# One PSUM tile per bank and attention outputs in halves, in a planned attention and token/channel mixing kernel

## The chip, the cores and the metric

The kernel runs on one core of one Trainium2 chip. The metric is device time in microseconds (us), as the median of several runs. A profile's span is about two us shorter than the time of its run. Engines in the profile: PE is TensorE, PEld its weight loads, DVE is VectorE, ACT is ScalarE, POOL is GpSimd, SP issues DMAs (POOL issues the loads).

## The reference, cut to what matters

```python
# 8 batches, 8 heads, 1024 rows, head size 64, projection 64
k_proj = einsum('ks,bhsd->bhkd', E, k);  v_proj = einsum('ks,bhsd->bhkd', F, v)
x = softmax(q @ k_proj.T / 8) @ v_proj             # [8, 1024, 512] after joining heads
h = relu(x.T @ w_tok1) @ w_tok2                    # token mixing, hidden 256
u = x + h.T
out = u + relu(u @ w_ch1) @ w_ch2                  # channel mixing, hidden 1536
```

In the program, `token1` and `token2` are the two products of the token mixing; `kp` and `vb` are the copies of the projected k and v, `x_sb` holds x and `uT` the transpose of u. The two channel products take most of TensorE's work. The kernel computes them with seven block products in place of eight (Strassen's scheme), so partial results live in PSUM banks that are seeded by a copy and added to.

## The kernel before: the parts that matter

A planner written in Python orders the whole program before it is built. It has three streams that take PSUM banks: U (the up products), D (the down products) and F (the "front": projections, scores, attention outputs "attend", token mixing). U and D share banks 0 to 5, F has banks 6 and 7. The planner knows eight single banks. The program declares four tiles of two banks each:

```python
pairs = [ps.tile([P, 2, S2], F32, tag=f"ps{i}", name=f"ps{i}") for i in range(4)]

def bank(b):
    t = pairs[b.at[0] // 2]
    return t if b.n == 2 else t[:, b.at[0] % 2, :]
```

The waits between engines are added later by the framework, which follows the accesses of each tile.

`attend` writes a head's output to both front banks and VectorE normalises it in one reciprocal and one product:

```python
def attend(h, due):
    bk = Bank("F", 2)                       # both front banks
    ...                                     # 4 matmuls, 130 columns each
    nc.vector.reciprocal(out=rdn, in_=view()[:, :, :, D])
    nc.vector.tensor_tensor(out=x_sb[...], in0=view()[:, :, :, 0:D],   # 512 columns
                            in1=rdn[..., None].to_broadcast([P, 2, 4, D]), op=ALU.mult)
```

The projections of k and v stand in one bank and leave it in four copies, `kp` twice and `vb` twice, shared between VectorE and ScalarE.

The softmax here doesn't subtract the row's maximum and nothing guards it: scores larger than these inputs give would overflow.

Of the kernel before, what the change touches and what calls it, by code (L numbers as in the profile page):

```python
# [25 lines left out]
class Bank:  # L26


    def __init__(self, stream, n=1):
        self.stream, self.n, self.jobs, self.at = stream, n, [], None  # L30
        self.read, self.write = [], []


class Planner:
# [35 lines left out]
    def plan(self):  # L70
# [30 lines left out]

        def home(b, now):

            if held[b.stream] + b.n > self.caps[b.stream]:
                return None
            if b.stream != "F" and turn[b.stream][0] is not b:
                return None
            best = None
            if b.n == 1:
                spots = [(i,) for i in ((6, 7) if b.stream == "F" else range(6))]  # L110
            else:
                spots = [(6, 7)]
            for s in spots:
                t = [bank_free[i] for i in s]
                if None in t:
                    continue
                mates = 0
                c = (max(now, max(t)), -mates, max(t), s)
                if best is None or c < best:
                    best = c  # L120
            return best

        while any(can.values()):
            pick = None
            for e, js in can.items():
                f = free.get(e, 0.0)
                cands = []
                for j in js:
                    t = max(f, est[j.n])
                    spot = None  # L130
                    if j.takes:
                        h = home(j.takes[0], t)
                        if h is None:
                            continue
                        t, spot = h[0], h[3]
                    cands.append((t, j.prio, j.n, j, spot))
                if not cands:
                    continue
                t0 = min(c[0] for c in cands) + 0.02
                c = min((c for c in cands if c[0] <= t0), key=lambda c: (c[1], c[2]))  # L140
                if pick is None or c[0] < pick[0]:
                    pick = c
            if pick is None:
                raise RuntimeError("no job can go on", [(j.eng, j.fn.__qualname__, j.prio) for js in can.values() for j in js][:20], held, bank_free)
            t, _, _, j, spot = pick
            can[j.eng].remove(j)
            j.start, j.end, j.full = t, t + j.lat, t + j.lat + 0.03
            free[j.eng] = t + j.occ
            if j.takes:
                b = j.takes[0]  # L150
                b.at = spot
                turn[b.stream].remove(b)
                held[b.stream] += b.n
                for i in spot:
                    bank_free[i] = None
            for b in j.banks:
                left[id(b)] -= 1
                if not left[id(b)]:
                    held[b.stream] -= b.n
                    for i in b.at:  # L160
                        bank_free[i] = max(x.end for x in b.jobs) + 0.1
            order.append(j)
            for s in j.next:
                waiting[s.n] -= 1
                if not waiting[s.n]:
                    open_(s)
# [5 lines left out]
def kernel(  # L172
# [13 lines left out]
    nc = tc.nc  # L186
# [40 lines left out]
    def tile_of(shape, dtype, name):  # L227
        return sb.tile(shape, dtype, tag=name, name=name)

    pairs = [ps.tile([P, 2, S2], F32, tag=f"ps{i}", name=f"ps{i}") for i in range(4)]  # L230

    def bank(b):

        t = pairs[b.at[0] // 2]
        return t if b.n == 2 else t[:, b.at[0] % 2, :]

    ident = tile_of([P, P], BF16, "ident")
    make_identity(nc, ident)
# [25 lines left out]
    S_t = [tile_of([P, 4, 2, 2, P], BF16, f"S{i}") for i in range(2)]  # L264
    G_t = [tile_of([P, 7, C2, 2 * P], BF16, f"G{i}") for i in range(2)]
    a_t = [tile_of([P, S2], BF16, f"a{i}") for i in range(4)]
    rdn_t = [tile_of([P, 2, 4], F32, f"rdn{i}") for i in range(4)]
    ub_t = [tile_of([P, 2, 2 * P], F32, f"ub{i}") for i in range(2)]
    ua_t = [tile_of([P, 2, 2 * P], F32, f"ua{i}") for i in range(2)]
    g21_t = [tile_of([P, 2, 2 * P], BF16, f"g21{i}") for i in range(2)]  # L270
# [98 lines left out]
    def warm(i):  # L369
        pe(  # L370
            1, 512,
            lambda: blank(pairs[i // 2][:, i % 2, :]),
            prio=-200, writes=[("bank", i)],
        )

# [50 lines left out]
    def kv_proj(b, h0, hn, due):  # L426
        hs = slice(h0, h0 + hn)
        heads = range(h0, h0 + hn)
        bk = Bank("F")

        def view():
            return bank(bk).rearrange("p (h d) -> p h d", d=D)

        def mm(lo, hi):
            t = view()
            for si in range(lo, hi):
                a, z = si == 0, si == NSI - 1
                nc.tensor.matmul(  # L438
                    t[0:KP, 0:hn], ET_sb[:, si, :], k_sb[:, hs, si, :], start=a, stop=z
                )  # L440
                nc.tensor.matmul(
                    t[KP : 2 * KP, 0:hn], FT_sb[:, si, :], v_sb[:, hs, si, :], start=a, stop=z
                )

        cols = hn * D
        reads = ["ET", "FT"] + [(n, h) for n in "kv" for h in heads]
        pl.add(
            "PE", 8 * max(cols, 128) / 2400 + 0.22, 8 * max(cols, 128) / 2400 + 0.22,
            lambda: mm(0, NSI), reads=reads, takes=[bk], prio=due,
            after=[("vb", i, h) for i in range(2) for h in heads],  # L450
        )
        e = [
            lambda: nc.vector.tensor_copy(out=kp[:, hs, 0, :], in_=view()[0:KP, 0:hn]),
            lambda: nc.scalar.copy(out=kp[:, hs, 1, :], in_=view()[0:KP, 0:hn]),
            lambda: nc.vector.tensor_copy(
                out=vb[KP : 2 * KP, hs, 1, 0:D], in_=view()[KP : 2 * KP, 0:hn]
            ),
            lambda: nc.scalar.copy(out=vb[0:KP, hs, 0, 0:D], in_=view()[KP : 2 * KP, 0:hn]),
        ]
        dve(cols, e[0], writes=[("kp", 0, h) for h in heads], uses=[bk])  # L460
        act(cols, e[1], writes=[("kp", 1, h) for h in heads], uses=[bk])
        dve(cols, e[2], writes=[("vb", 1, h) for h in heads], uses=[bk])
        act(cols, e[3], writes=[("vb", 0, h) for h in heads], uses=[bk])

    def k_transpose(h0, hn, due):
# [77 lines left out]
            writes=[("a", h % 4)], uses=[bk],  # L543
        )

    def attend(h, due):
        bk = Bank("F", 2)

        def view():
            return bank(bk)[:, :, 0 : 4 * D1].rearrange("p n (c d) -> p n c d", d=D1)  # L550

        def mm():
            for j in range(NJ):
                nc.tensor.matmul(  # L554
                    view()[:, j // 2, 2 * (j % 2) : 2 * (j % 2) + 2].rearrange("p c d -> p (c d)"),
                    a_t[h % 4][:, j * P : (j + 1) * P],
                    vb[:, h].rearrange("k c d -> k (c d)"), start=True, stop=True,
                )

        pe(  # L560
            NJ, 130, mm, reads=[("a", h % 4), ("vb", 0, h), ("vb", 1, h)], takes=[bk], prio=due,
            after=[("x", h)],
        )
        rdn = rdn_t[h % 4]
        pl.add(
            "DVE", 0.23, 0.21,
            lambda: nc.vector.reciprocal(out=rdn, in_=view()[:, :, :, D]),
            writes=[("rdn", h % 4)], uses=[bk],
        )
        dve(  # L570
            512,
            lambda: nc.vector.tensor_tensor(  # L572
                out=x_sb[:, :, h * D : (h + 1) * D].rearrange("p (n c) d -> p n c d", n=2),
                in0=view()[:, :, :, 0:D],
                in1=rdn[:, :, :, None].to_broadcast([P, 2, 4, D]),
                op=ALU.mult,
            ),
            reads=[("rdn", h % 4)], writes=[("x", h)], uses=[bk],
        )

    def token1(t, due):
# [8 lines left out]

        for part in range(2):
            pe(
                4, 512, lambda part=part: mm(part), reads=["wt1"] + [("x", h) for h in range(H)],
                takes=[bk] if part == 0 else [], uses=[bk] if part else [], prio=due + 0.9 * part,
            )
        act(
# [4 lines left out]
    def token2(b, si, due):  # L601
        bk = Bank("F")

        def mm():
# [12 lines left out]
            lambda: nc.vector.tensor_add(  # L617
                out=u_t[b % 2][:, si, :], in0=bank(bk), in1=x_sb[:, si, :]
            ),
            reads=[("x", h) for h in range(H)], writes=[("u", b % 2, si)], uses=[bk],  # L620
        )
        if si % NJ == NJ - 1:
            i = si // NJ
# [30 lines left out]
    def token1_pair(hp, due):  # L654
# [13 lines left out]
        for t in range(TC):  # L668
            pe(
                NSI, 128, lambda t=t: mm(t),  # L670
                reads=["wt1", ("x", 2 * hp), ("x", 2 * hp + 1)],
                takes=[bk] if t == 0 else [], uses=[bk] if t else [], prio=due,
            )
        act(
# [5 lines left out]
    def token2_pair(hp, i, due):  # L680
# [6 lines left out]
        def mm():  # L687
# [14 lines left out]
            lambda: nc.vector.tensor_add(  # L702
                out=u_t[0][:, rows, cols], in0=view(), in1=x_sb[:, rows, cols]
            ),
            reads=[("x", 2 * hp), ("x", 2 * hp + 1)], writes=[("up", hp, i)], uses=[bk],
        )

    def u_transpose_pe(hp, i, due):
# [230 lines left out]
    for hp in range(HP):  # L939
        q_transpose_pe(hp, due + 8 + 2 * hp)  # L940
        scores(2 * hp, due + 9 + 2 * hp)
        scores(2 * hp + 1, due + 9 + 2 * hp)
        attend(2 * hp, due + 10 + 2 * hp)
        attend(2 * hp + 1, due + 10 + 2 * hp)
    for hp in range(HP):
        token1_pair(hp, due + 20 + hp)
    for i in range(2):
# [4 lines left out]
    def front(b, begin, end):  # L952
# [4 lines left out]
        for h in range(H):  # L957
            if h + 2 < H:
                units.append((0.4, lambda t, h=h: scores(h + 2, t)))
            units.append((0.5, lambda t, h=h: attend(h, t)))  # L960
        for n in range(TC):
            units.append((1.8, lambda t, n=n: token1(n, t)))
        for si in range(NSI):
# [60 lines left out]
```

## Time and profile before

| | before |
|---|---|
| time, median | 560.0 us |
| PE / DVE / ACT busy | 82 / 58 / 42% |
| idle gaps of PE | 100.2 us (558.8 - 458.6) |
| one steady batch | 58.3 us (first token1 matmul of one batch to that of the next, mean of six) |

The page of before: engine busy time, then the clock granted to TensorE in 40 slices of the span, in tenths (9 is full or nearly so).

```profile
span 558.8 us, 9128 instructions
...
PE 458.6 (82%) x3692; PEld 346.7 (62%) x3692; DVE 325.7 (58%) x656; ACT 234.9 (42%) x428; POOL 106.7 (19%) x122
...
PE   5555467888789989888888898989899889988995
...
PEclk8567577998799999999999999999999999999998
```

PE is never full for long, and in the first sixth it is about half idle.

The windows view of before: the first 90 us, and one steady batch. Columns are the length, the busy time of each engine with its instruction count, the granted clock, the DMA share and GB/s.

```profile
0.00:90.00 90.00, 50.62 (x396) 35.20 (x397) 35.49 (x79) 20.00 (x42) 28.24 (x44) 0.67 0.94 153
235.50:294.80 59.30, 51.08 (x423) 39.16 (x422) 38.23 (x75) 27.52 (x49) 11.77 (x12) 1.00 0.68 122
```

In a steady batch 8.2 of 59.3 us are gaps of PE.

The waits view of before, PE alone: who waited, for whom, us in total, times, longest.

```profile
PE ps L554 <- DVE x_sb L572: 9.6, 12, 2.5
PE ps L475 <- DVE vb L455: 8.6, 7, 2.3
PE ps L869 <- ACT G L796: 7.5, 10, 1.7
PE ps L606 <- DVE u L617: 5.4, 15, 0.6
...
PE ps L869 <- ACT ps L815: 3.3, 8, 0.7
```

L869 is a down product, L815 the copy that seeds an up bank. The timeline of before shows one such wait (start, length, engine, line; in brackets the idle time before and what ended it):

```profile
272.79 0.60 PE L775 MATMUL ps<-uT,wT 128*128 128x256 bf16 x4
...
273.48 0.57 ACT L815 COPY ps<-ps 128x512 f32<-128x512 f32 x1 [0.78 <-PE ps L775]
274.10 0.82 PE L869 MATMUL ps<-wT,G 128*128 128x256 bf16 x6 [0.71 <-ACT ps L815]
```

By the program, this copy reads bank 4 and this down product writes bank 5, the other bank of the pair. The tile makes the wait, not the data (e2 below makes each bank a tile, leaves the plan and is 73.9 us faster). I call it a neighbour wait below. The program of before has 277 waits of PE on an instruction that shares a pair tile with it but no bank; read out of the program and set against the trace, they end 62.9 us of PE's gaps. (A recount that takes in the shortest gaps gives 279 waits and 65.1 us.)

### The profile page before, as it was taken

How to read it: one execution, taken by the hardware profiler on the slowest of the kernel's cores; microseconds unless marked ns; L12 is line 12 of the kernel's file. 1: busy time of each engine (PE TensorE's matmuls, PEld its weight loads, DVE VectorE, ACT ScalarE, POOL GpSimd, SP SyncE). 2: the span in 40 equal slices, each digit the busy share in tenths (PEclk: the TensorE clock that was granted, in tenths of full speed). 3: DMA queues.
4: the chain of work that ended last, by engine and by line, in shares of the span. 5: the costliest groups of instructions: out<-in, count | busy, mean ns of one | idle time of the engine just before them, and what ended most of it. 6: DMA issues, size and time to landing. Idle time of an engine off the chain costs nothing.

```text
span 558.8 us, 9128 instructions
## 1 busy us (share of the span) xinstructions
PE 458.6 (82%) x3692; PEld 346.7 (62%) x3692; DVE 325.7 (58%) x656; ACT 234.9 (42%) x428; POOL 106.7 (19%) x122
## 2 busy tenths in 40 slices
PE   5555467888789989888888898989899889988995
PEld 3424434655566667666766677667776676767874
DVE  2354434674476766656674658476856666655551
ACT  1222025542364366435543465346543653344541
POOL 7440030022021122104030312121101010011022
PEclk8567577998799999999999999999999999999998
DMA  8999529625945299637954497429632301222111
GB/s 134 206 201 206 99 47 187 107 39 89 227 87 126 39 174 167 109 80 121 182 99 93 76 178 161 114 38 192 116 109 39 113 1 76 39 35 80 77 76 76
DMA packets 93674, 61.67 MB, mean 110 GB/s; under 512 B 59840, under 2 KB 89024, under 8 KB 93632
## 3 DMA queue, kind: packets, MB, share of 16 engines
q0 software_dynamic: 30784, 29.63, 34.6%
q1 hardware_dynamic: 62848, 31.46, 23.7%
q8 instruction: 29, 0.48, 0.3%
q14 instruction: 13, 0.11, 0.1%
HBM read 59.24 MB, written 16.78 MB: 136 GB/s over the span
## 4 chain that ended last, share of the span: by engine, by line
PE 52%; DVE 20%; ACT 13%; DMA 10%; issue 4%; POOL 0%; DVEq 0%; ACTq 0%; POOLq 0%
PE ps L869 17%; PE ps L775 16%; DMA uT<-u 9%; PE ps L606 4%; PE ps L586 4%; DVE u L617 4%; DVE x_sb L572 2%; PE ps L438 2%; PE ps L533 2%; ACT ps L815 2%; DVE g L756 2%; DVE S L645 2%; ACT G L796 2%; DVE G L809 2%; DVE G L756 2%
## 5 line engine op out<-in xcount | busy, mean ns | idle before, releaser
L869 PEld LDWEIGHTS <-G 128*128 128x128 bf16 x1344 | 131.1, 98 | 46.4 <-issue 27.4
L869 PE MATMUL ps<-wc_sb,G 128*128 128x256 bf16 x768 | 104.7, 273 | 13.0 <-ACT G L796 6.1
L796 ACT ACTIVATE G<-ps 128x512 bf16<-128x512 f32 x96 | 57.4, 598 | 100.5 <-PE ps L775 92.4
L775 PEld LDWEIGHTS <-wc_sb 128*128 128x128 bf16 x768 | 74.5, 99 | 38.0 <-issue 22.3
L869 PE MATMUL ps<-wT,G 128*128 128x256 bf16 x576 | 78.8, 274 | 5.5 <-ACT ps L907 1.4
L775 PEld LDWEIGHTS <-wT 128*128 128x128 bf16 x576 | 56.7, 99 | 24.9 <-issue 13.7
L775 PE MATMUL ps<-uT,wc_sb 128*128 128x256 bf16 x384 | 59.8, 280 | 8.3 <-DVE g L756 3.5
L901 POOL TENSOR_TENSOR db<-db,u 128x512 f32<-128x512 f32 x16 | 19.1, 1191 | 237.8 <-ACT db L899 237.8
L617 DVE TENSOR_TENSOR u<-ps,x_sb 128x512 bf16<-128x512 f32 x56 | 37.5, 689 | 42.2 <-PE ps L606 40.3
L775 PE MATMUL ps<-S,wc_sb 128*128 128x256 bf16 x384 | 58.4, 275 | 3.6 <-DVE G L756 1.9
L901 POOL TENSOR_TENSOR o<-o,u 128x512 f32<-128x512 f32 x32 | 37.1, 1160 | 123.1 <-ACT o L899 117.7
L775 PE MATMUL ps<-S,wT 128*128 128x256 bf16 x384 | 57.0, 278 | 3.8 <-ACT ps L907 1.0
L756 DVE CUSTOM_DVE_ANT_0 g<-ps,ub 128x512 bf16<-128x512 f32 x48 | 33.0, 688 | 39.1 <-PE ps L775 12.7
L756 DVE CUSTOM_DVE_ANT_0 G<-ps,ua 128x512 bf16<-128x512 f32 x48 | 33.0, 688 | 37.1 <-ACT ua L802 25.6
L542 ACT ACTIVATE a<-ps 128x512 bf16<-128x512 f32 x64 | 36.5, 600 | 24.4 <-PE ps L533 24.4
L572 DVE TENSOR_TENSOR x_sb<-ps,rdn 128x512 bf16<-128x512 f32 x64 | 44.2, 691 | 2.0
L809 DVE TENSOR_TENSOR G<-G 128x512 bf16<-128x512 bf16 x96 | 43.4, 452 | 2.5
L802 ACT COPY ua<-ps 128x512 f32<-128x512 f32 x48 | 28.2, 588 | 32.9 <-PE ps L775 27.0
L606 PE MATMUL ps<-hT_sb,wt_sb 128*128 128x512 bf16 x112 | 32.5, 385 | 8.0 <-DVE u L617 5.4
L554 PE MATMUL ps<-vb,a 128*128 128x130 bf16 x256 | 26.2, 228 | 12.1 <-DVE x_sb L572 9.6
L815 ACT COPY ps<-ps 128x512 f32<-128x512 f32 x48 | 27.7, 578 | 17.4 <-PE ps L775 8.7
L802 ACT COPY ub<-ps 128x512 f32<-128x512 f32 x48 | 28.1, 585 | 10.9 <-PE ps L869 4.4
(72 smaller groups left out, 522.8 us busy)
## 6 DMA issues: line engine op xcount, KB each, us to landing
out_dram<-o SPq DMA_DIRECT2D x32, 512.0 KB, 3.3
k_sb<-in_k_dram POOLq DMA_DIRECT2D x14, 512.0 KB, 7.3
v_sb<-in_v_dram POOLq DMA_DIRECT2D x14, 512.0 KB, 9.3
q_sb<-in_q_dram POOLq DMA_DIRECT2D x14, 512.0 KB, 7.6
wc_sb<-in_moe_w_ch_dram POOLq DMA_DIRECT2D x6, 256.0 KB, 12.6
wc_sb<-in_moe_w_ch_dram POOLq DMA_DIRECT2D x4, 384.0 KB, 12.0
k_sb<-in_k_dram POOLq DMA_DIRECT2D x4, 256.0 KB, 7.6
v_sb<-in_v_dram POOLq DMA_DIRECT2D x4, 256.0 KB, 8.2
```

The lines of the kernel that those rows point to most:

```text
L542: lambda: nc.scalar.activation(out=a_t[h % 4], in_=bank(bk), func=ACT.Exp, scale=scale),
L572: lambda: nc.vector.tensor_tensor(out=x_sb[:, :, h * D : (h + 1) * D].rearrange("p (n c) d -> p n c d", n=2), in0=view()[:, :, :, 0:D], in ...
L606: nc.tensor.matmul(bank(bk), wt2_sb[:, t, si::NSI], hT_sb[:, t, :], start=(t == 0), stop=(t == TC - 1),)
L617: lambda: nc.vector.tensor_add(out=u_t[b % 2][:, si, :], in0=bank(bk), in1=x_sb[:, si, :]),
L756: nc.vector._custom_dve(TENSOR_ADD_SAT, out=out, in0=in0, in1=in1, s0=FMAX, s1=0.0)
L775: nc.tensor.matmul(t[:, c, :], w1_of(n, dd, 2 * m + c), a_of(j, n, dd), start=(n in (1, 7) and c == 0 and dd == 0), stop=(c == 1 and dd == 1),
L796: lambda: nc.scalar.activation(out=G[:, n, cs], in_=view(src), func=ACT.Relu),
L802: 512, lambda: nc.scalar.copy(out=dst, in_=view("y")), writes=[(name, s % 2)],
L809: 512, lambda: f(out=G[:, n, cs], in0=in0, in1=in1), ps=False, reads=deps,
L815: 512, lambda: nc.scalar.copy(out=view("y"), in_=view("x")), takes=[bk["y"]],
L869: nc.tensor.matmul(view(X_OF[n])[:, t, :], G[:, G_OF[n], cc, t * P : (t + 1) * P], w2_of(n, cc), start=(n in (1, 7) and t == 0 and cc == 0 ...
L901: 512, lambda: nc.gpsimd.tensor_add(out=dst, in0=dst, in1=u_of(sh, dh)),
```

## The change

Every bank becomes a tile of its own. `attend` is cut into two halves that take one bank each. The two copies of `kp` go to VectorE and the two of `vb` to ScalarE.

```diff
-    pairs = [ps.tile([P, 2, S2], F32, tag=f"ps{i}", name=f"ps{i}") for i in range(4)]
+    banks = [ps.tile([P, S2], F32, tag=f"ps{i}", name=f"ps{i}") for i in range(8)]
     def bank(b):
-        t = pairs[b.at[0] // 2]
-        return t if b.n == 2 else t[:, b.at[0] % 2, :]
+        return banks[b.at]
 ...                                    # kv_proj
-            lambda: nc.scalar.copy(out=kp[:, hs, 1, :], in_=view()[0:KP, 0:hn]),
-            lambda: nc.vector.tensor_copy(
+            lambda: nc.vector.tensor_copy(out=kp[:, hs, 1, :], in_=view()[0:KP, 0:hn]),
+            lambda: nc.scalar.copy(
                 out=vb[KP : 2 * KP, hs, 1, 0:D], in_=view()[KP : 2 * KP, 0:hn]
 ...
-    def attend(h, due):
-        bk = Bank("F", 2)
+    def attend(h, half, due):
+        bk = Bank("F")
 ...                                    # 2 matmuls, a reciprocal of 4, a product of 256 columns
-            512,
+            256,
-                out=x_sb[:, :, h * D : (h + 1) * D].rearrange("p (n c) d -> p n c d", n=2),
+                out=x_sb[:, 4 * half : 4 * half + 4, h * D : (h + 1) * D],
 ...                                    # readers of x name the halves they need;
 ...                                    # the planner loses its two-bank case
```

More of the change, by code (lines that the diff above doesn't have):

```diff
@@ L26, with __init__ @@
 class Bank:
-    def __init__(self, stream, n=1):
-        self.stream, self.n, self.jobs, self.at = stream, n, [], None
+    def __init__(self, stream):
+        self.stream, self.jobs, self.at = stream, [], None
         self.read, self.write = [], []
@@ L102, in home @@
         def home(b, now):
-            if held[b.stream] + b.n > self.caps[b.stream]:
+            if held[b.stream] == self.caps[b.stream]:
                 return None
@@ L108, in home @@
             best = None
-            if b.n == 1:
-                spots = [(i,) for i in ((6, 7) if b.stream == "F" else range(6))]
-            else:
-                spots = [(6, 7)]
-            for s in spots:
-                t = [bank_free[i] for i in s]
-                if None in t:
-                    continue
-                mates = 0
-                c = (max(now, max(t)), -mates, max(t), s)
-                if best is None or c < best:
-                    best = c
+            for i in (6, 7) if b.stream == "F" else range(6):
+                t = bank_free[i]
+                if t is not None and (best is None or (max(now, t), t, i) < best):
+                    best = (max(now, t), t, i)
             return best
@@ L134, in plan @@
                             continue
-                        t, spot = h[0], h[3]
+                        t, spot = h[0], h[2]
                     cands.append((t, j.prio, j.n, j, spot))
@@ L152, in plan @@
                 turn[b.stream].remove(b)
-                held[b.stream] += b.n
-                for i in spot:
-                    bank_free[i] = None
+                held[b.stream] += 1
+                bank_free[spot] = None
             for b in j.banks:
@@ L158, in plan @@
                 if not left[id(b)]:
-                    held[b.stream] -= b.n
-                    for i in b.at:
-                        bank_free[i] = max(x.end for x in b.jobs) + 0.1
+                    held[b.stream] -= 1
+                    bank_free[b.at] = max(x.end for x in b.jobs) + 0.1
             order.append(j)
@@ L266 @@
     a_t = [tile_of([P, S2], BF16, f"a{i}") for i in range(4)]
-    rdn_t = [tile_of([P, 2, 4], F32, f"rdn{i}") for i in range(4)]
+    rdn_t = [tile_of([P, 4], F32, f"rdn{i}") for i in range(4)]
     ub_t = [tile_of([P, 2, 2 * P], F32, f"ub{i}") for i in range(2)]
@@ L371, in warm @@
             1, 512,
-            lambda: blank(pairs[i // 2][:, i % 2, :]),
+            lambda: blank(banks[i]),
             prio=-200, writes=[("bank", i)],
@@ L460, in kv_proj @@
         dve(cols, e[0], writes=[("kp", 0, h) for h in heads], uses=[bk])
-        act(cols, e[1], writes=[("kp", 1, h) for h in heads], uses=[bk])
-        dve(cols, e[2], writes=[("vb", 1, h) for h in heads], uses=[bk])
+        dve(cols, e[1], writes=[("kp", 1, h) for h in heads], uses=[bk])
+        act(cols, e[2], writes=[("vb", 1, h) for h in heads], uses=[bk])
         act(cols, e[3], writes=[("vb", 0, h) for h in heads], uses=[bk])
@@ L544, in scores @@
         )
-    def attend(h, due):
-        bk = Bank("F", 2)
+    def attend(h, half, due):
+        bk = Bank("F")
+        rdn = rdn_t[2 * (h % 2) + half]
         def view():
-            return bank(bk)[:, :, 0 : 4 * D1].rearrange("p n (c d) -> p n c d", d=D1)
+            return bank(bk)[:, 0 : 4 * D1].rearrange("p (c d) -> p c d", d=D1)
         def mm():
-            for j in range(NJ):
+            for jj in range(2):
+                j = 2 * half + jj
                 nc.tensor.matmul(
-                    view()[:, j // 2, 2 * (j % 2) : 2 * (j % 2) + 2].rearrange("p c d -> p (c d)"),
+                    view()[:, 2 * jj : 2 * jj + 2].rearrange("p c d -> p (c d)"),
                     a_t[h % 4][:, j * P : (j + 1) * P],
@@ L558, in mm @@
                 )
+        key = ("rdn", 2 * (h % 2) + half)
         pe(
-            NJ, 130, mm, reads=[("a", h % 4), ("vb", 0, h), ("vb", 1, h)], takes=[bk], prio=due,
-            after=[("x", h)],
+            2, 130, mm, reads=[("a", h % 4), ("vb", 0, h), ("vb", 1, h)], takes=[bk], prio=due,
+            after=[("x", h, half)],
         )
-        rdn = rdn_t[h % 4]
         pl.add(
-            "DVE", 0.23, 0.21,
-            lambda: nc.vector.reciprocal(out=rdn, in_=view()[:, :, :, D]),
-            writes=[("rdn", h % 4)], uses=[bk],
+            "DVE", 0.14, 0.18, lambda: nc.vector.reciprocal(out=rdn, in_=view()[:, :, D]),
+            writes=[key], uses=[bk],
         )
         dve(
-            512,
+            256,
             lambda: nc.vector.tensor_tensor(
-                out=x_sb[:, :, h * D : (h + 1) * D].rearrange("p (n c) d -> p n c d", n=2),
-                in0=view()[:, :, :, 0:D],
-                in1=rdn[:, :, :, None].to_broadcast([P, 2, 4, D]),
+                out=x_sb[:, 4 * half : 4 * half + 4, h * D : (h + 1) * D],
+                in0=view()[:, :, 0:D],
+                in1=rdn[:, :, None].to_broadcast([P, 4, D]),
                 op=ALU.mult,
             ),
-            reads=[("rdn", h % 4)], writes=[("x", h)], uses=[bk],
+            reads=[key], writes=[("x", h, half)], uses=[bk],
         )
@@ L592, in token1 @@
             pe(
-                4, 512, lambda part=part: mm(part), reads=["wt1"] + [("x", h) for h in range(H)],
+                4, 512, lambda part=part: mm(part), reads=["wt1"] + [("x", h, part) for h in range(H)],
                 takes=[bk] if part == 0 else [], uses=[bk] if part else [], prio=due + 0.9 * part,
@@ L619, in token2 @@
             ),
-            reads=[("x", h) for h in range(H)], writes=[("u", b % 2, si)], uses=[bk],
+            reads=[("x", h, si // NJ) for h in range(H)], writes=[("u", b % 2, si)], uses=[bk],
         )
@@ L670, in token1_pair @@
                 NSI, 128, lambda t=t: mm(t),
-                reads=["wt1", ("x", 2 * hp), ("x", 2 * hp + 1)],
+                reads=["wt1"] + [("x", 2 * hp + h, n) for h in range(2) for n in range(2)],
                 takes=[bk] if t == 0 else [], uses=[bk] if t else [], prio=due,
@@ L704, in token2_pair @@
             ),
-            reads=[("x", 2 * hp), ("x", 2 * hp + 1)], writes=[("up", hp, i)], uses=[bk],
+            reads=[("x", 2 * hp, i), ("x", 2 * hp + 1, i)], writes=[("up", hp, i)], uses=[bk],
         )
@@ L942 @@
         scores(2 * hp + 1, due + 9 + 2 * hp)
-        attend(2 * hp, due + 10 + 2 * hp)
-        attend(2 * hp + 1, due + 10 + 2 * hp)
+        for h in (2 * hp, 2 * hp + 1):
+            for half in range(2):
+                attend(h, half, due + 10 + 2 * hp)
     for hp in range(HP):
@@ L959, in front @@
                 units.append((0.4, lambda t, h=h: scores(h + 2, t)))
-            units.append((0.5, lambda t, h=h: attend(h, t)))
+            for half in range(2):
+                units.append((0.25, lambda t, h=h, half=half: attend(h, half, t)))
         for n in range(TC):
```

## The prediction

The recorded text is cut in three places: an estimate of the VectorE work that the halves add, the marks that followed from it, and a sentence on banks, none of which a run then on record showed. No term of the sum is cut: 560 - 54 - 5 = 501 stands, and a quarter taken off the gain of 59 us leaves 44 and so 516; the estimate had entered only as one reason for that quarter.

> **What bounds the kernel now.** TensorE with its stalls. The page gives PE 82% busy of a 558.8 us span, VectorE 58%, ScalarE 42%. The windows view shows a steady state: every 59-60 us stretch (one batch) from 149 to 446 us holds 52 to 55 us of PE work, 37 to 40 of VectorE, 28 to 29 of ScalarE. The first 90 us hold only 51 us of PE work. PE's idle gaps sum to about 94 us.
>
> I set the trace against the waits in the program of the kernel before, and asked which PSUM bank the waiting instruction and the awaited one touch. Of 448 waits of PE over PSUM, 277 are on an instruction that touches only the *other* bank of the same two-bank tile. By traced idle time, 62.9 us of PE's gaps (124 of them) end with such a neighbour-bank wait, 22.0 us with a real one. Example in the timeline: at 274.10 us a down product had idled 0.71 us until a ScalarE copy (an up bank's seed) ended, of which it uses nothing. The waits view has the largest forms: k transpose behind the vb eviction (8.6 us, 7 times), down products behind relu G (7.5), token2 behind a neighbour's u eviction (5.4).
>
> [...]
>
> **What the change does.** One tile per bank removes the neighbour waits on all engines. With all else at its traced time, real dependencies would leave 8.6 of the 62.9 us: 14.5 us go before 90 us, 39.7 after. Each stop also costs a refill (6 matmuls take 0.82 us in a lone group, 18 take 2.14: roughly 0.1 us): about 5 us more.
>
> Attend halves take one bank each, not both, so scores and attends overlap. Cost: 128 reciprocals and 128 products on VectorE for 64 and 64. A 512-column product takes 691 ns, a reciprocal 202[...].
>
> kv eviction: two VectorE reads, then two on ScalarE, so the k transpose starts after about 1.4 us instead of 2.7.
>
> **Sum.** First order: 560 - 54 - 5 = 501. Not all is kept: at 53-54 us a batch VectorE is some 75% loaded, in-order queues and two F banks form new real waits, the DMA transposes stay (9-11 us, on the chain once a batch), and the start (DMA 93% busy before 90 us) can shorten only by 6-10 us. I expect about three quarters, 44 us. **516 us, 80% range 498 to 537.** Faster by over 2%: 0.94, within 2%: 0.05, slower: 0.01.
>
> **What would show it.** Steady batches of 53-55 us; PE gaps down to 45-55 us, hardly any on a bank that the waiter doesn't touch; the first batch's products starting 5-10 us earlier;[...] matmul counts unchanged.
>
> **What would make it wrong.** New real waits of PE on VectorE (attend halves, two F banks) that eat the gain; the planner's new order, which I can't see; a start bound by its loads; or neighbour waits that hid slack, so that gaps only move.

## More of the kernel before

"Half clock" means a stretch in which the profile shows a granted TensorE clock of 0.5.

The order of each engine's instructions is the plan's, and the trace of before shows that order: its 3692 matmuls, its 651 VectorE and its 427 ScalarE instructions (memsets and the table load left out) stand, line for line, as in the built program.

## The result, and the profile after

| | before | after |
|---|---|---|
| time, median | 560.0 us | 475.7 us (473.4 to 480.1, 4 runs) |
| ratio | | 0.850 (95% interval 0.843 to 0.857) |
| idle gaps of PE | 100.2 us | 46.7 us |
| one steady batch | 58.3 us | 50.3 us |

A ratio here is the mean time of one kernel's fast runs over that of the other's of the same rounds, so it is not quite the ratio of the medians quoted beside it. The time lies 22 us below the predicted range; the predicted gain was 44 us and the measured one is 84.

The page of after:

```profile
span 471.6 us, 9198 instructions
...
PE 424.9 (90%) x3665; PEld 338.9 (72%) x3692; DVE 326.7 (69%) x784; ACT 235.3 (50%) x428; POOL 107.2 (23%) x122
...
PE   4757889992999989999999999999999999999994
...
PEclk8576999997999999999999999999999999999999
```

The gaps fell by 53.5 us. The other 33.7 us came off PE's *busy* time, although all 3692 matmuls are still run (their weight loads are counted in full; 27 matmul records are missing in this trace, and a run of the same speed that has them all, e4 below, shows 31.2 us less busy and 56.3 us less idle). That is the surprise to explain.

The windows view of after, for the same two stretches:

```profile
0.00:90.00 90.00, 68.50 (x627) 51.35 (x631) 58.12 (x157) 37.97 (x76) 32.06 (x48) 0.85 1.14 183
237.10:289.30 52.20, 50.00 (x430) 40.08 (x432) 39.19 (x94) 28.74 (x51) 11.05 (x12) 1.00 0.74 142
```

The gaps of PE in a steady batch are 2.2 us now. By 90 us PE has done 627 matmuls where it had done 396. The transfers speed up too, 183 GB/s for 153, so they had not been at their limit in the start. (The DMA share of this view is no ceiling either: it was 0.94 and is 1.14.)

The waits view of after, PE alone:

```profile
PE ps L765 <- DMA uT<-u: 8.5, 1, 8.5
PE ps L464 <- DVE kp L443: 7.6, 9, 1.3
PE ps L522 <- DVE x_sb L562: 5.0, 8, 1.8
PE ps L545 <- DVE x_sb L562: 4.7, 11, 0.9
```

The waits of products (L765, L859, the old L775 and L869) on ScalarE and VectorE are nearly gone (32 us in all before, 2.8 after, 5.7 in e4), and the program has no neighbour wait left. The timeline shows a seed copy (L805, the old L815) and a product in the neighbouring bank; by the program this copy reads bank 5 and this product writes bank 4:

```profile
249.31 0.57 ACT L805 COPY ps<-ps 128x512 f32<-128x512 f32 x1
...
249.57 0.60 PE L765 MATMUL ps<-uT,wT 128*128 128x256 bf16 x4
```

The product starts in the middle of the copy. The groups of attend's VectorE work, before and then after (busy, mean ns of one, idle time before and its causes):

```profile
L572 DVE TENSOR_TENSOR x_sb<-ps,rdn 128x512 bf16<-128x512 f32 x64 | 44.2, 691 | 2.0
...
L567 DVE RECIPROCAL rdn<-ps 128x8 f32<-128x8 f32 x64 | 13.0, 202 | 15.6 <-PE ps L554 15.3 <-ACT ps L815 0.3
```

```profile
L562 DVE TENSOR_TENSOR x_sb<-ps,rdn 128x256 bf16<-128x256 f32 x128 | 50.8, 415 | 0.9
...
L557 DVE RECIPROCAL rdn<-ps 128x4 f32<-128x4 f32 x128 | 21.6, 175 | 15.9 <-PE ps L545 13.8 <-ACT a L531 1.1 <-ACT ua L792 0.8
```

Count times mean: 57.1 us before, 75.5 after, so +18.4. VectorE's busy time as the page gives it, a union of overlapping records, rises only from 325.7 to 326.7; the plain sum of all its records rises by 16, from 352 to 368.

### Where busy time can hide a stop

The groups of both kernels say that a 256-column matmul is recorded for 273 ns. The timeline of before shows six matmuls after which PE stops, and six that run straight into the next ones:

```profile
280.24 0.82 PE L869 MATMUL ps<-wc_sb,G 128*128 128x256 bf16 x6
...
282.16 0.60 PE L775 MATMUL ps<-S,wc_sb 128*128 128x256 bf16 x4 [1.10 <-DVE G L756]
...
282.82 0.82 PE L869 MATMUL ps<-wc_sb,G 128*128 128x256 bf16 x6
...
283.48 0.60 PE L775 MATMUL ps<-uT,wT 128*128 128x256 bf16 x4
```

Both sixes are recorded for 0.82 us, but in the second the next matmul starts 0.66 us after the first of the six. The chain of waits of after (start, length, what) counts a group only up to the next start:

```profile
87.60 0.66 PE ps L859 x6
...
418.65 1.31 PE ps L859 x12
```

Twelve in 1.31 us are 109 ns each, and six are 0.66 us. In the six that stop, the record of the last one runs on for 165 ns (273 - 108) after the next matmul could have started. When PE stops, this tail counts as busy. The stop above cost 1.26 us (1.92 - 0.66), of which the profile shows 1.10 as idle. A stop that shows a gap is therefore its visible gap *plus* 165 ns; a stop shorter than the tail shows no gap at all. (The profiler models the ends of matmuls, so the split into gap and tail rests on its model; their sum rests on starts alone.)

So I made an account of every trace from the *starts* of successive matmuls: issue time at full clock, what it takes longer in stretches at half clock, visible gaps, and the rest, which is hidden in busy time. A stop is any start over 40 ns late. The projections of k and v need care: their matmuls start in pairs, in before most often 3 ns apart (31 ns in the median) and the next pair some 213 ns later, and this is their normal pace. (A first account took some 49 of these pairs in each trace for stops of about 0.21 us each; this table is made without them, and the differences between the kernels hardly changed. The 18.6 us in the expectation of i1 are of the first account.) Traces with all 3692 matmuls are used; for the kernel after, the run with the kv copies put back stands in, whose time is the same (474.1 us, below).

| kernel | stops | with a visible gap | issue | more at half clock | visible gaps | hidden | hidden per stop with a gap |
|---|---|---|---|---|---|---|---|
| before | 248 | 191 | 401.6 | 18.2 | 91.7 | 38.5 | 0.168 |
| six stream banks split | 137 | 91 | 401.4 | 17.8 | 62.6 | 21.2 | 0.170 |
| two front banks split | 232 | 169 | 401.5 | 14.0 | 72.3 | 35.2 | 0.166 |
| all banks split, attend whole | 155 | 63 | 402.2 | 8.5 | 41.7 | 20.7 | 0.177 |
| after (kv put back) | 125 | 71 | 401.7 | 7.0 | 35.4 | 18.3 | 0.171 |
| after on pair tiles | 297 | 211 | 401.7 | 12.1 | 99.6 | 45.3 | 0.170 |

All in us. The kernels of the middle rows are the experiments that follow. From before to after: visible gaps -56.3, hidden -20.2, half clock -11.1, issue unchanged. Hidden time and half clock sum to 31.3 us, which is what PE's busy time fell by.

### The profile page after: what moved, and what is told of

It is laid out like the page before. It is cut to its first block, busy times and chain, and to the rows that moved or that the text cites. A ratio compares the mean times of both kernels' runs of the same rounds, so it can differ in the third digit from the quotient of the medians.

```text
span 471.6 us, 9198 instructions
## 1 busy us (share of the span) xinstructions
PE 424.9 (90%) x3665; PEld 338.9 (72%) x3692; DVE 326.7 (69%) x784; ACT 235.3 (50%) x428; POOL 107.2 (23%) x122
## 4 chain that ended last, share of the span: by engine, by line
PE 63%; DVE 16%; DMA 13%; ACT 3%; issue 2%; POOL 2%; DVEq 0%; POOLq 0%; ACTq 0%
PE ps L765 23%; PE ps L859 22%; DMA uT<-u 11%; PE ps L576 5%; PE ps L596 4%; DVE S L635 3%; DVE G L799 3%; DVE x_sb L562 2%; DMA q_sb<-in_q_dram 2%; PE ps L545 2%; PE ps L427 2%; PE ps L522 2%; PE ps L653 1%; DVE G L746 1%; DVE u L607 1%
## 5 line engine op out<-in xcount | busy, mean ns | idle before, releaser
L859 PEld LDWEIGHTS <-G 128*128 128x128 bf16 x1344 | 130.8, 98 | 22.0 <-issue 1.8
L859 PE MATMUL ps<-wc_sb,G 128*128 128x256 bf16 x768 | 104.5, 273 | 1.2 <-DVE da L907 1.1
L765 PEld LDWEIGHTS <-wc_sb 128*128 128x128 bf16 x768 | 72.8, 98 | 28.4 <-issue 12.5
L859 PE MATMUL ps<-wT,G 128*128 128x256 bf16 x576 | 78.1, 273 | 0.1
L765 PE MATMUL ps<-uT,wc_sb 128*128 128x256 bf16 x384 | 58.0, 274 | 8.8 <-DMA uT<-u 8.5
L765 PEld LDWEIGHTS <-wT 128*128 128x128 bf16 x576 | 55.4, 98 | 14.5 <-issue 4.5
L765 PE MATMUL ps<-S,wc_sb 128*128 128x256 bf16 x384 | 57.6, 273 | 1.3 <-ACT ua L792 1.0
L765 PE MATMUL ps<-S,wT 128*128 128x256 bf16 x384 | 54.9, 274 | 0.0
L562 DVE TENSOR_TENSOR x_sb<-ps,rdn 128x256 bf16<-128x256 f32 x128 | 50.8, 415 | 0.9
L531 ACT ACTIVATE a<-ps 128x512 bf16<-128x512 f32 x64 | 37.8, 599 | 24.9 <-PE ps L522 24.8
L545 PE MATMUL ps<-vb,a 128*128 128x130 bf16 x256 | 34.0, 226 | 6.2 <-DVE x_sb L562 4.7
L545 PEld LDWEIGHTS <-a 128*128 128x128 bf16 x256 | 23.5, 100 | 17.4 <-issue 10.3
L805 ACT COPY ps<-ps 128x512 f32<-128x512 f32 x48 | 28.2, 588 | 10.5 <-PE ps L765 10.1
L557 DVE RECIPROCAL rdn<-ps 128x4 f32<-128x4 f32 x128 | 21.6, 175 | 15.9 <-PE ps L545 13.8
## 6 DMA issues: line engine op xcount, KB each, us to landing
wc_sb<-in_moe_w_ch_dram POOLq DMA_DIRECT2D x4, 384.0 KB, 12.1
```

What stands on the lines that cost most here:

```text
L531: lambda: nc.scalar.activation(out=a_t[h % 4], in_=bank(bk), func=ACT.Exp, scale=scale),
L545: nc.tensor.matmul(view()[:, 2 * jj : 2 * jj + 2].rearrange("p c d -> p (c d)"), a_t[h % 4][:, j * P : (j + 1) * P], vb[:, h].rearrange("k ...
L562: lambda: nc.vector.tensor_tensor(out=x_sb[:, 4 * half : 4 * half + 4, h * D : (h + 1) * D], in0=view()[:, :, 0:D], in1=rdn[:, :, None].to ...
L765: nc.tensor.matmul(t[:, c, :], w1_of(n, dd, 2 * m + c), a_of(j, n, dd), start=(n in (1, 7) and c == 0 and dd == 0), stop=(c == 1 and dd == 1),
L805: 512, lambda: nc.scalar.copy(out=view("y"), in_=view("x")), takes=[bk["y"]],
L859: nc.tensor.matmul(view(X_OF[n])[:, t, :], G[:, G_OF[n], cc, t * P : (t + 1) * P], w2_of(n, cc), start=(n in (1, 7) and t == 0 and cc == 0 ...
```

## The experiments

Each diff is against the kernel named. All runs gave the right result. A first submission of four runs found no chip; they were sent again, as f0 to f3.

My theory (A): neighbour waits are the whole gain, and they cost more than their gaps. The rival (B): my 44 us for the tiles were right, and the finer attend with its new plan brought the rest. Splitting the banks changes neither the plan nor the order of the instructions, so the two can be told apart.

### e1: six stream banks as tiles, the front left a pair

```diff
-    pairs = [ps.tile([P, 2, S2], ...) for i in range(4)]
+    banks = [ps.tile([P, S2], ...) for i in range(6)]
+    pair = ps.tile([P, 2, S2], F32, tag="ps6", name="ps6")
+    banks += [pair[:, 0, :], pair[:, 1, :]]
```

> The kernel before with the six banks of the up and down streams as tiles of their own; the two banks of the front (attention, token mixing) stay one pair tile. The plan and the order of all instructions are those of before; only waits go. Theory A (neighbour-bank waits are the whole gain; a stop of TensorE costs more than its visible gap): about 520 us (505 to 535), a good part of the 84 us, since about 28 of the 63 us of neighbour-wait gaps stand before up and down products, and the stops hide more. Theory B (the finer attend and the new plan give what went beyond the predicted 44 us): 535 us or more.

Measured: 514.4 us, ratio 0.923 (0.918 to 0.928), 44.5 us below the 558.9 of before in the same rounds. This alone, with each engine's work unchanged, is what I had predicted for everything. Its waits view has the front waits left:

```profile
PE ps L476 <- DVE vb L456: 10.6, 10, 2.3
PE ps L534 <- DVE x_sb L573: 8.8, 5, 4.0
PE ps L555 <- DVE x_sb L573: 8.3, 9, 2.5
```

### g1: only the two front banks as tiles

```diff
+    banks = [pairs[i // 2][:, i % 2, :] for i in range(6)]
+    banks += [ps.tile([P, S2], ...) for i in range(6, 8)]
     # attend as in e2, next
```

> The kernel before with only the two front banks as tiles of their own (attend whole, its VectorE work issued per bank); the six up and down banks stay pair tiles. Waits of TensorE on a neighbour bank that the program holds: 180, against 277 in before and 97 in the run that split the other six. If the two parts add up (44.5 us there, 74 us together): 525 to 535 us. If the gain is mostly where both streams mix: under 515 or over 545.

Measured: 533.6 us, ratio 0.952 (0.948 to 0.957), 26.5 us below before. In this run it is the product waits that are left:

```profile
PE ps L783 <- DVE g L764: 7.7, 6, 2.8
...
PE ps L877 <- ACT G L804: 7.0, 9, 1.7
```

### e2: all banks as tiles, attend whole, the plan of before

```diff
+    banks = [ps.tile([P, S2], ...) for i in range(8)]
 # attend: still one job on banks 6 and 7
-    nc.vector.reciprocal(out=rdn, in_=view()[:, :, :, D])
+    for n in range(2):
+        nc.vector.reciprocal(out=rdn[:, n], in_=view(n)[:, :, D])
 # the product likewise, once per bank
```

> The kernel before with all eight banks as tiles of their own, the plan of before: attend still takes both front banks at once, in one job; its reciprocal and product are issued once per bank, so VectorE has the 128 + 128 instructions of after. Theory A: 476 to 490 us, nearly the time of after. Theory B: 510 to 525 us.

Measured: 485.0 us, ratio 0.869 (0.865 to 0.873), 73.9 us below before. The two parts alone sum to 71. So theory B falls as the main cause: with the plan of before and attend whole, most of the 84 us are there, and VectorE already issues 128 + 128 instructions for attend. The halves with their new plan give the last 10 us or so (485.0 to 475.7); which of the two does it was not tested.

The spans can be cut at the first token1 matmul of batch 1 (120.9 us into the span of before). That stretch is the start; the rest is mostly steady.

| kernel | start | rest |
|---|---|---|
| before | 120.9 | 437.9 |
| e1, stream banks split | 111.3 | 400.6 |
| g1, front banks split | 99.8 | 432.1 |
| e2, all split | 95.9 | 386.0 |
| after | 88.2 | 383.4 |

The stream banks free the steady part (37 of 52 us that e2 gains there), the front banks the start (21 of 25). The halves shorten mostly the start again. (The plan of after cuts the work a little later: 618 matmuls stand before the cut there, 600 in the other plan. Single traces differ too: the same kernel after has a start of 91.0 us in f0.)

### e3: the kernel after on pair tiles

```diff
-    banks = [ps.tile([P, S2], ...) for i in range(8)]
+    pairs = [ps.tile([P, 2, S2], ...) for i in range(4)]
+    banks = [pairs[i // 2][:, i % 2, :] for i in range(8)]
```

> The kernel after, its plan and order unchanged, but its eight banks are views of four pair tiles again. Theory A: 545 to 580 us, no better than before or worse, since half-head jobs on one pair tile wait for each other. Theory B: 520 us or less.

Measured: 568.3 us, ratio 1.019 (1.014 to 1.024). Halves on pair tiles are 9 us slower than before: 336 neighbour waits of PE are in this program, against 277 (the recount: 356 against 279), and TensorE stops 297 times, against 248. So the halves are worth something only once the banks are tiles of their own.

### e4: the kv copies put back on the engines of before

The edit is the kv_proj part of the change, reversed.

> The kernel after with the four kv evictions back on the engines of before. Both theories: within 1% of after, 472 to 482 us. If the swap matters, over 482.

Measured: 474.1 us, ratio 0.852 (0.847 to 0.857), the same as after. The swap gains nothing. The traces even show it going the wrong way: with the copies put back, both `kp` copies of a full-size group are done 1.3 us after the first begins, where in after they take 2.6, and the k transpose waits 2.7 us for them in all, where in after it waits 7.6. The time is the same for all that. f3 looks at why they take longer.

### f0 to f3, on one chip

> The kernel after, unchanged, as the reference on this chip for the three runs that follow. All theories: 473 to 480 us.

Measured: 476.1 us, ratio 0.851 (0.848 to 0.853).

**f3, a vb copy after both kp copies.** In the trace of after the four copies still ran as kp, vb, vb, kp in ten of eleven groups: the planner does not know that the reads of one bank by two engines wait for each other (in the trace of after the second kp copy waits 11 times, 10.0 us in all, for a vb copy out of the same bank), and gave ScalarE its turn too early.

```diff
-        act(cols, e[2], writes=[("vb", 1, h) for h in heads], uses=[bk])
+        act(cols, e[2], reads=[("kp", 1, h) for h in heads],
+            writes=[("vb", 1, h) for h in heads], uses=[bk])
```

> The kernel after with one dependency more in the plan: the vb evictions follow the second kp eviction. In after the plan still put both ScalarE evictions between the two VectorE ones, so that the k transpose waited 7.6 us in all for the second kp copy. Expected: that wait under 3 us, and 3 to 6 us faster; if the wait only moves, within 2 us.

Measured: 474.0 us, ratio 0.847 (0.845 to 0.849). The edit did half of what I meant: it holds back one vb copy and not the other, and in the trace the copies ran as kp, vb, kp, vb, with both kp copies done after 2.0 us. The k transpose's wait on the second kp copy fell from 7.5 us to 3.0 against f0, while the scores' wait on x_sb rose from 4.9 to 7.0. The gain, 2 us, is at the edge of what these rounds resolve; most of the wait moved. The order kp, kp, vb, vb on these engines was never run.

**f1, matmuls of zeros at the start.** The account has 11.1 us less at half clock, so is the half clock a cost of its own? The half-clock stretches of before, without the one at the end, last 3.4, 6.8, 10.2, 17.1 and 20.5 us. In the 3.4 us before each of seven falls of before's clock (all but the one at the end), matmul records fill 40 to 45% of the time; in after they fill 52% and 53% before the first two falls and nothing before the third, which comes in the wait of 8.5 us.

```diff
         bank_free = [0.0] * 8
+        bank_free[5] = 44.0                  # bank 5 kept out of the plan's start
     for j in plan:
         j.fn()
+        if j.eng == "PE" and 2.0 < j.start < 43.0:
+            fill(...)                        # 256 to 2048 columns of zeros into bank 5
```

> The kernel after; in its first 43 planned us TensorE also runs matmuls of zeros into a bank kept free for them, so that its idle time there is filled. Clock theory (half-clock stretches come from an idle TensorE and cost time by themselves): half-clock time in the trace falls from 37.8 us to under 20, and the time falls by 3 to 6 us. Rival (the start is a chain of evictions and loads, and the clock follows it but costs nothing): no change within 2 us, or slower by what the fillers take, even if the clock rises.

Measured: 478.4 us, ratio 0.856 (0.854 to 0.859). Half-clock time fell from 39.7 us (f0) to 24.7, not to under 20 as expected, and the kernel was 2 us slower. The rival holds, but it is a weak test: there were only about 5 us to win, and keeping bank 5 free changes the start's plan as well. So I tried it on before too.

**i1, the same on the kernel before**, with 512 columns as the least filler and banks 4 and 5 kept free:

> The kernel before with matmuls of zeros after each TensorE job of its first 43 planned us, on a bank pair kept free for them. Half-clock time in the trace of before: 77 us, and its matmuls issue 18.6 us longer for it, 14.4 of them before the first token1. If the half clock is a loss of its own: half-clock time under 50 us and 4 to 9 us faster. If it only follows the idle time: within 3 us of before (559.9), or slower by the fillers.

Measured: 560.5 us, ratio 1.001 (0.995 to 1.006). The clock line of its page:

```profile
PEclk9988678998999999999999999999899999999999
```

Half-clock time fell from 77.1 us to 38.9, and the time did not move. So lifting the clock in this way gains nothing. Why is not shown; my reading is that the start is a chain of small steps between engines, in which matmuls are short. Less was at stake than the half-clock time suggests: in the start, the kernel's own matmuls took 13.9 us longer for the half clock in before and still 8.5 in i1. (The fillers take 12 us of issue themselves, mostly in former gaps, and the two banks kept free change the start's plan; a way to lift the clock without them was not tried.)

**f2, the first DMA transposes on TensorE.** After's longest wait is one of 8.5 us for a DMA transpose of u, issued among the loads of the next batch.

```diff
-        if si % NJ == NJ - 1:
+        if si % NJ == NJ - 1 and b == 1:
+            for hp in range(HP):
+                u_transpose_pe(hp, si // NJ, due, b)     # as batch 0 does it
+        elif si % NJ == NJ - 1:
             ...                                          # DMA transpose
```

> The kernel after, but the transposes of u for batch 1 alone run on TensorE and ScalarE and not by DMA. In the trace of after TensorE waits 8.5 us, its longest wait, for that DMA, which ran among the loads of batch 2, and the clock falls to half for 6.8 us. If that wait is real loss: 6 to 10 us faster. If the next stage is late for another reason: under 3 us.

Measured: 467.4 us, ratio 0.835 (0.832 to 0.837), 8.7 us below f0. The wait is gone. This version beats both kernels. Its longest wait is now a front one:

```profile
PE ps L522 <- DVE x_sb L562: 10.0, 7, 2.6
```

### g2, both mends

The edit is that of f2 and that of f3 together.

> The kernel after with both mends: the first DMA transposes of u moved to TensorE, and the vb evictions behind the second kp eviction. If the parts add: 8.7 and 2 us off the 476 us of after, 463 to 468 us.

Measured: 470.7 us, ratio 0.840 (0.836 to 0.844), outside the expected range. The mends do not add: this is no faster than f2 alone (0.832 to 0.837, in other rounds), the fastest version that I have.

### g3 and h1: does VectorE's load cost time?

The prediction took a quarter off the gain, VectorE's load the first of its reasons. g3 issues each reciprocal twice; h1 takes f2 and moves both kp copies to ScalarE as well.

```diff
-            "DVE", 0.14, 0.18, lambda: nc.vector.reciprocal(out=rdn, in_=view()[:, :, D]),
+            "DVE", 0.14, 0.18,
+            lambda: [nc.vector.reciprocal(out=rdn, in_=view()[:, :, D]) for _ in range(2)],
```

> The kernel after with each of its 128 reciprocals issued twice (same result): some 22 us of VectorE work more[...]. If VectorE's load near 70% turns into new waits of TensorE: 8 us slower or more. If it has the slack: under 4 us slower.

The recorded text is cut in one place, a clause on the estimate that is cut from the prediction too. The 22 us are 128 reciprocals of 175 ns, as measured in after.

Measured: 488.5 us, ratio 0.872 (0.869 to 0.875), 12 to 13 us slower than after (0.851 in f0, in other rounds). The front waits took it up; the lines that answer to those of after:

```profile
PE ps L522 <- DVE x_sb L562: 9.3, 12, 2.2
...
PE ps L545 <- DVE x_sb L562: 8.1, 17, 1.1
```

h1, against f2:

```diff
-            lambda: nc.vector.tensor_copy(out=kp[:, hs, 0, :], in_=view()[0:KP, 0:hn]),
+            lambda: nc.scalar.copy(out=kp[:, hs, 0, :], in_=view()[0:KP, 0:hn]),
 # kp[:, hs, 1, :] likewise, and both jobs planned for ScalarE
```

> The kernel after with the first DMA transposes of u on TensorE (467.4 us) and, besides, all four kv evictions on ScalarE: 11 us less on VectorE, 9 us more on ScalarE, and no change of engine within that bank. If VectorE's load costs time in both directions, as the doubled reciprocals did (12 us for 22 us): 3 to 7 us faster than 467, ratio to before 0.822 to 0.829. If it costs only where the attend chain gets longer: within 2 us of 467.

Measured: 468.8 us, ratio 0.837 (0.832 to 0.842): the same as f2. Taking VectorE work away outside the attend chain (busy 314.2 us for 324.7 in f2) gains nothing. Putting 22 us into that chain costs more than half of them. These two runs fit a chain that is bound by its own length, between two banks, better than a VectorE that is bound by its load; they differ in both place and amount, and h1 loads ScalarE with 8 us more, so they do not prove it.

## Why the prediction was wrong, point by point

In short: the mechanism was right, and terms of the sum were not. The refill was put at 5 us and measured 20, a cut of 15 us for new waits did not come, the start could shorten by 33 us and not by 6 to 10, and 11 us at half clock were left out.

**Right: the cause.** TensorE was held by waits that only the pair tiles made. e1, g1 and e2 show it with the plan unchanged, and e3 shows it from the other side.

**Right: the visible gaps.** "With all else at its traced time, real dependencies would leave 8.6 of the 62.9 us", so 54 us were to go; the account has 56. In e2, where waits went and the plan stayed, the gaps fell by 50.0; the halves brought the rest, so the agreement of 56 with 54 is in part luck. "PE gaps down to 45-55 us": 46.7, counted over the whole span. In the prediction's own count, which starts from 94 us and leaves out the end of the span, they are 41.0, somewhat lower than it said.

**Wrong, the refill.** "Each stop also costs a refill (6 matmuls take 0.82 us in a lone group, 18 take 2.14: roughly 0.1 us): about 5 us more." The numbers were there and were divided wrongly: twelve more matmuls take 1.32 us more, so six take 0.66, and the rest of the 0.82 is a tail of 0.16. (Even 0.1 us for each of 124 stops would have been 12, not 5.) The tail goes with every stop that shows a gap: 124 neighbour waits times 0.165 is 20.5 us, and the account measures 20.2, with 123 stops fewer, 120 of them with a gap. Short by 15 us.

**Wrong, the haircut.** "Not all is kept ... I expect about three quarters, 44 us." That took 15 us off a sum of 59. New real waits did come: after has waits of scores and attends on x_sb. But they took little: of the 54 us that real dependencies were to free, e2 has 50 with the old plan, and after has 56. What h1 measured fits a VectorE that at 69% had room outside the attend chain, and its busy time rose by 1 us only, to 326.7 (though the sum of its records did rise by 16). The fear was not empty in kind: 22 us more in the attend chain, which bring VectorE's busy time to 348.0 us, cost 12 (g3).

**Wrong, the start.** "... and the start (DMA 93% busy before 90 us) can shorten only by 6-10 us." It shortened by 32.7 us (120.9 to 88.2). A busy DMA was taken for a bound. The page of before shows that it wasn't busy all the time (DMA in tenths, slices of 14 us; the fifth and sixth slices have 5 and 2), and the waits view of all engines shows what the loads waited for, in before and then in after:

```profile
DMA  8999529625945299637954497429632301222111
...
POOL k_sb L308 <- PE ps L441: 40.0, 5, 37.6
```

```profile
DMA  8999999979393896649742998359522402241222
...
POOL k_sb L297 <- PE ps L430: 20.2, 4, 19.1
```

A load of k waited 37.6 us for the projection that frees its buffer, and 19.1 us in after, so the loads of the third batch began at 59.7 us where they had begun at 78.3. g1 shows the two front banks alone bringing 21 us of the start. One mark of the prediction failed the other way: the first up product starts only 1.7 us earlier (50.3 to 48.6 us), not 5 to 10.

**Left out: the clock.** Matmuls at half clock took 11.1 us less. As f1 and i1 gained nothing by lifting the clock, I read this as a part of the shorter start and not as a cause of its own. That is an argument from two runs that also carry their fillers and a changed plan, and they lifted only a part of it; it is not shown.

The sum: 560 - 56 - 20 - 11 = 473, where after has 475.7 and its stand-in 474.1. The terms of the miss of 40 us are the 15 us of refill, the 15 of haircut and the 11 at half clock; the start cuts across all three.

**Smaller points.** The 256-column product took 415 ns (the 512-column one 691) and the reciprocal of 4 columns 175 (that of 8 took 202). "... the k transpose starts after about 1.4 us" failed: the plan put vb between the two kp copies, and it stayed near 2.6 us (94.83 to 97.45 us in the trace of after). Steady batches were to take 53 to 55 us and take 50.3. With neighbouring banks in use at once, as in the timeline of after (249.31 us), the results stay right, and ScalarE's relu over a bank takes 597 ns after for 598 before.

## What to carry to other kernels

Declare each PSUM bank that is scheduled on its own as a tile of its own (559 us over pair tiles and 485 over single ones here, e2); where two banks share a tile, list the waits in the program whose two ends touch no common bank, and sum the gaps that they end. Count stops as well as gaps: in the trace's busy time each stop hides the tail of the last matmul (165 ns here), so cost stops from the starts of matmuls, not from idle time, and first learn the normal pace of each kind of matmul, pairs that run side by side above all. A busy DMA at the start does not show that the loads bind (here its share was 0.94, and the start still shortened by 32.7 us); look at what the loads themselves wait for.
